# A seventh V tile loaded in the middle of a fused attention-block kernel, with the homes of four operands exchanged

## The chip, the cores and the metric

The kernel runs on one core of a Trainium2 chip. The metric is the device time of one execution in microseconds (us), the median of three runs for the kernel before. One further execution was recorded by the profiler; all times of single instructions come from it, counted from the start of its span.

## The reference

The reference computes one decode step of a conditioned transformer block, and the gradients of its result. Cut to what matters:

```python
sa, ca, ga, sb, cb, gb = split(silu(c) @ w_mod, 6)          # 640 values each
h  = layernorm(x) * (1 + ca) + sa                           # x: 1 x 640
q  = (h @ wq)                                               # 32 heads x 192
p  = softmax(q . K * 192**-0.5)                             # K, V: 32 heads x 8192 x 192, bfloat16
x  = x + ga * ((p . V) @ wo)
h  = layernorm(x) * (1 + cb) + sb
x  = x + gb * mlp(h)       # x1 = h + const; x1 + gelu(layernorm(x1) @ w3) @ w4; w3: 640 x 1536, w4: 1536 x 640
out, and for a given grad_out the gradients of x, K, V, wq, wo, w3, w4, c, w_mod
```

K and V are 100 MB each, and so are their gradients dK and dV. For each head, dV is the outer product of the softmax row with the head's output gradient, and dK is the outer product of the score gradient dS with q. For dS the kernel needs the product of V with the output gradient, so V is read a second time.

## The kernel before, in words

**Tiles.** A head's K or V is handled as two tiles of 128 partitions x 32 rows x 192 values in bfloat16: 1536 KB each. The kernel has five K buffers (`KB`, 0 to 4), three V buffers (`VB`, 0 to 2), and `qs_bc`, the scaled queries of all heads on every partition, which is as large as a tile and is called `QT` when used as one. `pp` is a pool with one more buffer of that size, for products.

**First phase (to about 530 us).** A loop over 31 heads reads K and V of each head, makes scores, the softmax and the sums that the second phase needs.

**The middle (about 530 to 575 us).** The last head, the output projection, the MLP forward and backward. It is a long chain of small steps on all engines, written out by hand. In it `w3` is loaded into the product buffer (`wp`, L715) and its fifth row block into a `wo` buffer (`w3_4`); the rows of `w4` are loaded into `w4b` (blocks 0 to 3) and into `qs_bc` (blocks 4 to 11, L680). TensorE transposes `w3` block by block (`w3t`, L840), and the last of these transposes is the last reader of `w3`. `dg_part` (L533) reads all `w4` rows on VectorE; `h2_part` (L929) multiplies them with the activation `g_bf` on TensorE, 60 small matmuls, of which columns 0 and 1 are taken before the output gradient `dao` is known and columns 2 to 4 after it. `er` rows are the softmax rows, transposed and stored to a DRAM scratch `eT_d` (`e_rows_out`, L491 and L492), from which `load_er` (L367) brings 8 KB per tile back onto four partitions. Those of the first tile of the second phase (`er0`) are loaded into a free stretch of `qs_bc` (issued on the SP queue at 558.20), those of the second into a buffer of their own (`er_b`, 565.38). `m_add` (L481) is a small VectorE addition behind the `dao` chain; `er_b` lies where its operand `mt` was, so the load of `er_b` waits for it.

**The second phase (from 565 us).** A loop over 64 steps `s`, two tiles per head, from the last head down. A step makes dV of its tile from `er` and the head's output gradient (`dv_groups`: TensorE L1125, ScalarE copies L1126), and dK of its tile on VectorE (`dk_part`, L1130). For the next steps it multiplies the V tile with the output gradient (`mul_q`, L1095) and sums on TensorE (`tree_q`, L1114). Stores go out on the POOL queue (dV L1419, dK L1423), V tiles come in on the SP queue (L328), the er rows on the ACT queue. Outputs take turns in five buffers, V tiles in four:

```python
OB = (KC, VB[2], QT, KE, KD)                     # dV of step s: OB[2s % 5], dK: OB[(2s+1) % 5]
def v_buf(s):
    return KY if s == 0 else VB[2] if s == 1 else (VB[0], VB[1], KX, KY)[(s - 2) % 4]
```

V tiles 0 to 4 are in place or under way when the phase begins, tile 5 is loaded in two halves (L1433) as tile 0 is used up, and step `s` loads tile `s + 5` into the home of tile `s + 1` once that is multiplied. The order on TensorE, VectorE, ScalarE and SP is the order of the program text (a manual schedule); waits are put in by the tile framework wherever a buffer is written, read or given away. Weight gradients (`dw4`, dwo, dwq, dw_mod, dw3) and their loads (`wo` tiles L203, `wq` and `w_mod` chunks L1155) are placed between the steps by a plan written out by hand.

Of the kernel before, what the change touches and what calls it, by code (L numbers as in the profile page):

```python
# [8 lines left out]
FP32 = mybir.dt.float32  # L9
# [11 lines left out]
def kernel(  # L21
# [92 lines left out]
    def col(n, name, dtype=FP32):  # L114
        return const.tile([P, n], dtype, name=name)
# [238 lines left out]
    H1 = HQ - 1  # L354
    TL = NT - 1
    KX, KY, KC, KD, KE = (KB[(2 * HQ + k) % NKB] for k in (-4, -5, -3, -2, -1))
    OB = (KC, VB[2], QT, KE, KD)
    R8 = JH // 4
    NS = 2 * HQ

# [15 lines left out]
    with tc.tile_pool(name="vs", bufs=3) as vsp, tc.tile_pool(name="ft", bufs=2) as ft, \  # L376
# [161 lines left out]
        with tc.manual_schedule(engines=ORDER):  # L538
# [172 lines left out]
            score_tree(0, d1)  # L711
            score_mul(1, 1)
            score_tree(1, d1)
            wp = pp.tile([P, JH * DH], BF16, name="wp", tag="prod")
            nc.sync.dma_start(out=wp.rearrange("p (i n) -> p i n", i=4), in_=w3d[:, 0:4, :])  # L715
            dot_sum(d0, x["S"][:, 0:JH])
            o2 = pair_o(TL - 1, po)
# [5 lines left out]
            o_rows(H1 - 1, vy, op_y, 0, 16)  # L723
            w3_4 = wst.tile([P, F], BF16, name="w3_4", tag="wo")
            nc.sync.dma_start(out=w3_4, in_=w3d[:, 4, :])
            load_rows(qs_bc[:, 0 : 4 * D], 4, 8)
            load_rows(qs_bc[:, 4 * D : 8 * D], 8, 12)
            mx = row_max(x["S"])
            V_.tensor_copy(out=AO[:, :, 2 * TL - 2 : 2 * TL], in_=ps_ao)
            o_rows(H1 - 1, vy, op_y, 16, 48)  # L730
# [81 lines left out]
            ac = col(ND, "ac")  # L812
            V_.scalar_tensor_tensor(out=ac, in0=cb1, scalar=nm, in1=mo[:, 1, :], op0=ALU.mult, op1=ALU.add)
            e_rows_out(TL - 1, er_ps)
            e_rows_out(TL, er_ps2, qs_bc[:, 8 * D : 8 * D + P])
            er0 = load_er(0, nc.sync, qs_bc[:, 8 * D : 8 * D + R8 * P].rearrange("p (k q) -> p k q", q=P))
            v1, var2 = sc8[:, 8:9], sc8[:, 9:10]
            V_.scalar_tensor_tensor(out=v1, in0=va, scalar=r1[:, 0:1], in1=cov, op0=ALU.mult, op1=ALU.add)
            V_.scalar_tensor_tensor(out=var2, in0=v1, scalar=r1[:, 0:1], in1=k4[:, 3:4], op0=ALU.mult, op1=ALU.add)
# [104 lines left out]
            h2b = []  # L924

            def h2_part(lo, hi, a0=0, a1=NF):
                for k in range(lo, hi):
                    for a in range(a0, a1):
                        T_.matmul((h2_ps[:, k : k + 1] if k < 2 else h2b[0][:, k - 2 : k - 1]), lhsT=w4r(a)[:, k * P : (k + 1) * P], rhs=g_bf[:, a : a + 1], start=(a == 0), stop=(a == NF - 1))  # L929

            w3t()
            pe = m_units(3, ky[1], vs3, mp)
# [29 lines left out]
                    A_.activation(out=dst[:, (a - a0) * D : (a - a0 + 1) * D], in_=dbo_bc, func=ACT.Copy, scale=g_[:, a : a + 1])  # L962

            dw4s = w4b[:, 0 : 5 * D]
            dw4_act(dw4s, 0, 4, 5)
            dn_ps = psO.tile([P, 256], FP32, name="dn_ps", tag="op")[:, 0:ND]
            for a in range(NF):
                for k in range(ND):
# [18 lines left out]
            V_.tensor_tensor(out=Ag, in0=A1, in1=ga, op=ALU.mult)  # L987
            V_.scalar_tensor_tensor(out=B1, in0=vv, scalar=nr1, in1=dy_c, op0=ALU.mult, op1=ALU.add)
            V_.tensor_tensor(out=Bg, in0=B1, in1=ga, op=ALU.mult)
            pr = col(4 * ND, "pr").rearrange("p (a b) -> p a b", b=ND)  # L990
            V_.tensor_tensor(out=pr, in0=dn_ps[:, None, :].to_broadcast([P, 4, ND]), in1=G, op=ALU.mult)
            h2_part(0, 1, 0, 6)
            ps = mean_mm(pr.rearrange("p a b -> p (a b)"), 4 * ND)
            h2_part(0, 1, 6, NF)
            h2_part(1, 2)
            d_n2, vg = col(ND, "d_n2"), col(ND, "vg")
            V_.tensor_tensor(out=vg, in0=Ag, in1=dn_ps, op=ALU.mult)
            V_.tensor_tensor(out=vg, in0=vg, in1=Bg, op=ALU.add)
# [4 lines left out]
            V_.reduce_sum(out=qr, in_=q4.rearrange("p a b -> p b a"), axis=AX.X)  # L1003
            V_.tensor_tensor(out=dao_bf, in0=vg, in1=qr, op=ALU.add)
            V_.tensor_tensor(out=dao, in0=vg, in1=qr, op=ALU.add)
            m_add(H1 - 1, mp, mt)
            A_.copy(out=d_n2, in_=dn_ps)
            A_.copy(out=bo[:, 0:2], in_=h2_ps[:, 0:2])

            def dx1_out():  # L1010
                q = pr
# [15 lines left out]
                V_.tensor_scalar(out=x1, in0=mo[:, 0, :], scalar1=m0[:, 0:1], scalar2=None, op0=ALU.add)  # L1027


    cpr = col(HQ, "cpr")  # L1030
    ckS = col(NQ, "ckS")
    dha = col(ND, "dha")
# [30 lines left out]
                scale=rinv[:, h : h + 1],  # L1063
            )

    for t in (TL - 2, TL - 1):
        wo_l[t] = load_wo(t)
    er_l = {0: er0, 1: load_er(1, nc.sync)}

    def q_bc(h, pool=psB, tag="b"):  # L1070
        ps = pool.tile([P, 2 * P], FP32, name="q_ps", tag=tag)
# [5 lines left out]
    do_mm(TL, 1)  # L1077
    dw4_store(dw4s[:, 4 * D : 5 * D], 4, 1)
    dw4_act(dw4t, 5, 5, 6)
    h2b.append(psS.tile([P, 3], FP32, name="h2_pb", tag="s"))  # L1080
    h2_part(2, ND)
    cx = bst.tile([P, HQ, ND], FP32, name="v_bc")
    V_.tensor_tensor(out=cx, in0=AO.rearrange("p k h -> p h k"), in1=dao[:, None, :].to_broadcast([P, HQ, ND]), op=ALU.mult)
    cs = ckS[:, 0:HQ]
# [1 line left out]
    dw4_dve(dw4t, 5, 6, 7)  # L1086
    dw4_store(dw4t, 5, 2)
    qh = q_bc(H1, psT, "t")
    A_.copy(out=bo[:, 2:ND], in_=h2b[0])

    pq = pp.tile([P, 2, JQ, DH], BF16, name="pq", tag="prod")
    dao_bc = bst.tile([P, D], BF16, name="dao_bc")

    def mul_q(s, q):
# [168 lines left out]
    def g_small():  # L1263

        ck3 = ckS.rearrange("p (t b) -> p t b", b=3)
        V_.tensor_tensor(out=bo, in0=bo, in1=h_b, op=ALU.add)
        V_.tensor_tensor(out=ao, in0=aoP, in1=aoN, op=ALU.add)
        for b, h0 in ((0, 0), (2, 1)):
            V_.tensor_tensor(out=ck3[:, :, b], in0=M1[:, h0:HQ:2, DH], in1=cpr[:, h0:HQ:2], op=ALU.mult)
        for lo, hi, h0 in ((0, 64, 0), (64, P, 1)):  # L1270
            V_.tensor_tensor(out=ck3[lo:hi, :, 1], in0=M2[lo:hi, :, DH], in1=cpr[lo:hi, h0:HQ:2], op=ALU.mult)
        A_.mul(out=ckS, in_=ckS, mul=SCALE)
        V_.tensor_tensor(out=d_cb, in0=d_sb, in1=n1, op=ALU.mult)
        V_.tensor_tensor(out=d_ga, in0=dx1, in1=ao, op=ALU.mult)
# [112 lines left out]
        while prog[1] < NP and 4 * plan[prog[1]][0] <= prog[0] - 1:  # L1387
            step()

    def v_buf(s):  # L1390
        return KY if s == 0 else VB[2] if s == 1 else (VB[0], VB[1], KX, KY)[(s - 2) % 4]

    OL = [OB[i % 5] for i in range(2 * NS - 5)]
    OL += [v_buf(NS - 3), OB[3], v_buf(NS - 2), OB[4], v_buf(NS - 1)]
    v_l = {s: v_buf(s) for s in range(5)}
    assert ht(4) == (H1 - 2, 0) and v_buf(4) is KX
    dq_x = bst.tile([P, 3], FP32, name="dq_x")
    V_.memset(dq_x, 0.0)

# [61 lines left out]
    for s in range(NS):  # L1461
        h, t = ht(s)
        nxt = s + 1 < NS
        doh = do_of(h)
        dP = tcol(JH, "dP")
        dot_sum(ps, dP)
        dS4 = bst.tile([P, JH, 4], BF16, name="dS4", bufs=2)
        V_.scalar_tensor_tensor(
            out=dS4,
            in0=dP[:, :, None].to_broadcast([P, JH, 4]),  # L1470
            scalar=cpr[:, h : h + 1],
            in1=E_all[:, h, t * JH : (t + 1) * JH, None].to_broadcast([P, JH, 4]),
            op0=ALU.subtract,
            op1=ALU.mult,
        )
        dV, dK = OL[2 * s], OL[2 * s + 1]
        gs = [0, 1, 2, 3, 4, 5, 6, 7]
        if not nxt:
            gs = [0, 2, 4, 6, 1, 3, 5, 7]
        if s == 0:  # L1480
            gs = [None] * 8
        else:
            er = er_l.pop(s)
        if nxt:
            ps = psR.tile([P, JH, TS], FP32, name="dot_ps")

        def dv(k):
            if gs[k] is not None:
                dv_groups(dV, er, doh, (gs[k],))

        def tree(q, lo, hi):
            if nxt:
                tree_q(ps, s + 1, q, lo, hi)

        dv(0)
        dv(1)
        slot()
        tree(0, 0, 4)
        if nxt:
            mul_q(s + 1, 1)  # L1500
            half_q(s + 1, 1)
            v_l.pop(s + 1, None)
        if 0 < s < NS - 5:
            v_l[s + 5] = load_v(*ht(s + 5), v_buf(s + 5))
        dv(2)
        tree(0, 4, 8)
        dv(3)
        tree(0, 8, 12)
        dk_part(dK, qh, dS4, 0, JQ)
        if not nxt:  # L1510
            dv_store(s, dV, 0, JQ, nc.sync)
        if s in (0, NS - 1):
            dk_store(s, dK, 0, JQ)
        if s == 0:
            dw4_store(dw4s[:, 3 * D : 4 * D], 3, 1)
        slot()
        dv(4)
        tree(1, 0, 3)
        dk_part(dK, qh, dS4, JQ, JH)
        if s > 0 and late0:  # L1520
            late0.pop(0)()
        dk_store(s, dK, JQ if s in (0, NS - 1) else 0, JH)
        if row is not None:
            dq_cols(row)
            row = None
        dv(5)
        tree(1, 3, 6)
        slot()
        dv(6)
        tree(1, 6, 9)  # L1530
        dv(7)
        if s + 2 < NS:
            er_l[s + 2] = load_er(s + 2)
        if s == 0:
            pass
        elif nxt:
            dv_store(s, dV, 0, JH)
        else:
            dv_store(s, dV, JQ, JH, nc.sync)
        tree(1, 9, 12)  # L1540
        if h == H1:
            row = dq_rows(t, (KD, KE)[t], dS4)
        if s + 2 < NS:
            assert (s + 2) // 4 in done
            mul_q(s + 2, 0)
            half_q(s + 2, 0)
        if nxt and ht(s + 1)[0] != h:
            qh = q_bc(ht(s + 1)[0])
        done_s[0] = s + 1
        slot()  # L1550
# [32 lines left out]
```

## Time and profile before

| | |
|---|---|
| runs | 1386.55, 1388.25, 1389.93 us; median 1388.25 |
| profiled execution | 1387.89 us, its span 1386.1 us |
| busy: PE, DVE, ACT, POOL | 85%, 80%, 66%, 8% of the span |
| moved by DMA | 569.38 MB, 411 GB/s over the span |
| HBM read, written | 340.97 MB, 226.44 MB |

PE is TensorE, DVE VectorE, ACT ScalarE, POOL GpSimd, SP the engine that issues most loads. In the profile's rows a number in brackets is the idle time just before an instruction and what ended it. SPq and ACTq mark the issue of a transfer, not its end. In tables of stretches, each engine has its busy time and a count of instructions, PEclk is the share of TensorE's clock that was granted, and the last two columns are the busy share of the 16 DMA engines and the GB/s that they moved.

### The profile page before, as it was taken

The page shows a single profiled execution, that of the slowest core. Times are in us where ns is not written, and L with a number is a line of the kernel's source. Part 1 is how long each engine was busy: PE and PEld are TensorE (multiplying, and loading weights), DVE is VectorE, ACT ScalarE, POOL GpSimd, SP SyncE. Part 2 cuts the span into 40 slices and gives each one's busy share as a digit, 9 for nine tenths or more (in the row PEclk, how much of TensorE's full clock was granted, in tenths as well). Part 3 has the DMA queues.
Part 4 walks back from the last instruction along what each step waited for, and adds up shares of the span by engine and source line. Part 5 has one row for each costly group of instructions (what it writes and reads, how often), then busy time and mean ns, then how long its engine had stood idle before and what let it go on. Part 6 is the DMA issues. An engine that isn't in the chain of part 4 may idle for free.

```text
span 1386.1 us, 30498 instructions
## 1 busy us (share of the span) xinstructions
PE 1177.9 (85%) x12712; PEld 739.7 (53%) x12712; DVE 1111.0 (80%) x1459; ACT 910.1 (66%) x2003; POOL 108.5 (8%) x196
## 2 busy tenths in 40 slices
PE   3888999999999999989878799798778877878984
PEld 2777777777777778644323344344334343434431
DVE  4999999999999999988667587677677765877784
ACT  0777777777777778766556566566566565656654
POOL 0000000000000000111111011011011111111110
PEclk7899999999999999765555555555565565655555
DMA  9999999999999999799999999999999999999997
GB/s 382 389 415 415 419 423 425 407 426 421 421 415 423 406 421 384 286 413 423 422 424 419 422 410 428 425 420 426 422 408 421 417 423 422 397 420 417 424 416 336
DMA packets 76872, 569.38 MB, mean 411 GB/s; under 512 B 7422, under 2 KB 25198, under 8 KB 37182
## 3 DMA queue, kind: packets, MB, share of 16 engines
q1 hardware_dynamic: 51594, 342.03, 60.3%
q0 software_dynamic: 24624, 224.89, 38.8%
q8 instruction: 99, 1.62, 0.4%
q10 hardware_dynamic: 516, 0.51, 0.1%
q14 instruction: 39, 0.32, 0.1%
HBM read 340.97 MB, written 226.44 MB: 409 GB/s over the span
## 4 chain that ended last, share of the span: by engine, by line
issue 41%; DVE 24%; DMA 16%; PE 10%; POOL 5%; ACT 2%; POOLq 0%; SPq 0%; DVEq 0%; ACTq 0%
DMA KB<-in_A_k_cache_dram 10%; DVE prod L333 10%; DVE prod L337 5%; DMA out_dram<-KB 4%; DVE vs L403 3%; PE mp L425 2%; DMA out_dram<-VB 2%; POOL out_dram L1423 2%; PE half_ps L343 2%; POOL out_dram L1419 2%; PE mp L430 1%; PE dot_ps L1114 1%; POOL out_dram L1229 1%; DVE pq L1095 1%; ACT vs L410 1%
## 5 line engine op out<-in xcount | busy, mean ns | idle before, releaser
L1114 PE MATMUL dot_ps<-pq,ident_bf 128*128 128x256 bf16 x1494 | 377.4, 395 | 32.7 <-DVE dP L347 29.1
L1126 ACT CAST KB<-dv_ps 128x768 bf16<-128x768 f32 x312 | 242.9, 807 | 100.3 <-PE dv_ps L1125 99.4
L410 ACT ACTIVATE vs<-VB,Ef 128x192 bf16<-128x192 bf16 x840 | 303.6, 447 | 0.0
L1114 PEld LDWEIGHTS <-ident_bf 128*128 128x128 bf16 x1494 | 149.8, 123 | 185.4 <-issue 147.4
L1125 PE MATMUL dv_ps<-do_r,er_b 1*128 1x192 bf16 x2016 | 226.7, 336 | 4.2 <-ACT KB L1126 2.9
L333 DVE TENSOR_TENSOR prod<-KB,qs_bc 128x6144 bf16<-128x6144 bf16 x62 | 207.9, 3353 | 24.6 <-DMA KB<-in_A_k_cache_dram 20.8
L1130 DVE TENSOR_TENSOR KB<-qh,dS 128x3072 bf16<-128x3072 bf16 x74 | 128.1, 1752 | 101.1 <-DMA out_dram<-KB 91.6
L425 PE MATMUL mp<-vs,KB 128*128 128x193 bf16 x1984 | 189.3, 247 | 4.3 <-ACT vs L410 3.3
L425 PEld LDWEIGHTS <-KB 128*128 128x128 bf16 x1984 | 169.0, 98 | 13.4 <-issue 4.8
L1125 PEld LDWEIGHTS <-er_b 1*128 1x128 bf16 x2016 | 69.0, 104 | 148.1 <-issue 145.8
L904 ACT COPY wT<-wT_ps 128x1024 bf16<-128x1024 bf16 x82 | 79.3, 967 | 95.1 <-PE wT_ps L903 95.1
L343 PE MATMUL half_ps<-prod,ident_bf 128*128 128x256 bf16 x744 | 95.1, 279 | 43.2 <-DVE prod L337 43.2
L403 DVE TENSOR_TENSOR vs<-VB,E 128x1728 bf16<-128x1728 bf16 x120 | 123.7, 1051 | 0.3 <-ACT vs L410 0.3
L1095 DVE TENSOR_TENSOR pq<-VB,do_r 128x3072 bf16<-128x3072 bf16 x66 | 115.4, 1749 | 0.0
L337 DVE TENSOR_TENSOR prod<-prod 128x3072 bf16<-128x3072 bf16 x62 | 108.7, 1754 | 1.0
L1095 DVE TENSOR_TENSOR pq<-KB,do_r 128x3072 bf16<-128x3072 bf16 x62 | 108.5, 1749 | 0.0
L430 PE MATMUL mp<-vs,KB 128*64 128x193 bf16 x1968 | 105.7, 250 | 0.0
L343 PEld LDWEIGHTS <-ident_bf 128*128 128x128 bf16 x744 | 72.7, 99 | 61.5 <-issue 52.5
L1126 ACT CAST qs_bc<-dv_ps 128x768 bf16<-128x768 f32 x104 | 80.6, 805 | 31.2 <-PE dv_ps L1125 30.6
L390 ACT ACTIVATE E<-S_h,negm 128x256 bf16<-128x256 f32 x31 | 15.7, 508 | 114.1 <-DVE negm L561 111.8
L1126 ACT CAST VB<-dv_ps 128x768 bf16<-128x768 f32 x96 | 74.4, 807 | 24.4 <-PE dv_ps L1125 24.1
L430 PEld LDWEIGHTS <-KB 128*64 128x64 bf16 x1968 | 78.8, 109 | 19.9 <-issue 19.6
(383 smaller groups left out, 1214.3 us busy)
## 6 DMA issues: line engine op xcount, KB each, us to landing
VB<-in_A_v_cache_dram SPq DMA_DIRECT2D x93, 1536.0 KB
out_dram<-KB POOLq DMA_DIRECT2D x74, 1536.0 KB, 17.0
KB<-in_A_k_cache_dram SPq DMA_DIRECT2D x63, 1536.0 KB
KB<-in_A_v_cache_dram SPq DMA_DIRECT2D x29, 1536.0 KB
out_dram<-qs_bc POOLq DMA_DIRECT2D x25, 1536.0 KB, 16.4
out_dram<-VB POOLq DMA_DIRECT2D x25, 1536.0 KB, 16.6
wo_st<-in_A_wo_dram SPq DMA_DIRECT2D x31, 480.0 KB
w_st<-in_A_wq_dram SPq DMA_DIRECT2D x12, 960.0 KB
```

What stands on the lines that cost most here:

```text
L333: V_.tensor_tensor(out=prod, in0=src, in1=vec[:, None, :].to_broadcast([P, JH, DH]), op=ALU.mult)
L337: V_.tensor_tensor(out=prod[:, :, 0:HW], in0=prod[:, :, 0:HW], in1=prod[:, :, DH - HW : DH], op=ALU.add)
L343: T_.matmul(ps, lhsT=ident_bf, rhs=prod[:, :, k : k + TF], start=(k == 0), stop=(k == w - TF))
L403: V_.tensor_tensor(out=vs[:, 0:n, 0:DH].rearrange("p j (a b) -> p j a b", b=4), in0=v[:, v0 : v0 + n, :].rearrange("p j (a b) -> p j a b", ...
L410: A_.activation(out=vs[:, k, 0:DH], in_=v[:, v0 + k, :], func=ACT.Copy, scale=Ef[:, j0 + k : j0 + k + 1])
L425: T_.matmul(mp[:, 0:MW], lhsT=kb[:, j0 + k, 0:P], rhs=vs[:, k, 0:MW], start=(q == 0 and k == 0), stop=(z and k == JQ - 1), skip_group_chec ...
L430: T_.matmul(mp[p0 : p0 + 64, MO : MO + MW], lhsT=kb[:, j0 + k, P:DH], rhs=vs[:, k, 0:MW], start=False, stop=(z and k >= JQ - 2), skip_grou ...
L1095: V_.tensor_tensor(out=pq[:, q], in0=v_l[s][:, q * JQ : (q + 1) * JQ, :], in1=do_of(ht(s)[0])[:, None, :].to_broadcast([P, JQ, DH]), op=AL ...
L1114: T_.matmul(ps[:, q * JQ : (q + 1) * JQ, :], lhsT=ident_bf, rhs=pq[:, q, :, k : k + TS], start=(k == 0), stop=(k == w - TS), skip_group_ch ...
L1125: T_.matmul(ps[:, b, k * DH : (k + 1) * DH], lhsT=er[p0 : p0 + 1, 2 * m + k, :], rhs=doh[p0 : p0 + 1, :], start=True, stop=True)
L1126: A_.copy(out=dV4[:, 2 * q : 2 * q + 2, m * PW : (m + 1) * PW], in_=ps[:, :, 0:PW])
L1130: V_.tensor_tensor(out=dK[:, lo:hi, :].rearrange("p j (a b) -> p j a b", b=4), in0=qh.rearrange("p (a b) -> p a b", b=4)[:, None, :, :].to ...
```

## The change

- `w3` is loaded into `qs_bc` (home of q), and `w4` blocks 4 to 11 into the product buffer (`pq`, now allocated in the middle): the two exchange homes.
- Once the last transpose has read `w3`, the seventh V tile (`s = 6`) is loaded into `qs_bc`, between the loads of the two `wo` tiles. Step 1 of the second phase then loads no V tile.
- The homes are rotated: `qs_bc` joins the V buffers in place of `VB[0]`, and `VB[0]` the output buffers: `OB = (KC, VB[2], KE, VB[0], KD)`. V tile 2 still lies in `VB[0]`.
- `er0` is no longer loaded early into `qs_bc`: it goes with the second tile's, into an `er_b` buffer, issued behind the V tile and the second `wo` tile. For this `m_add` moves ahead of the `dao` chain's last steps.
- `h2_part` is divided by rows, not by columns: blocks 4 to 7 for all five columns before `dao`, the other eight blocks after it, into a second PSUM tile, copied to `bo2` and added later. One `dw4_act` (ScalarE) moves behind the copy of `bo`.

```diff
-    OB = (KC, VB[2], QT, KE, KD)
+    OB = (KC, VB[2], KE, VB[0], KD)
...
-            wp = pp.tile([P, JH * DH], BF16, name="wp", tag="prod")
+            pq = pp.tile([P, 2, JQ, DH], BF16, name="pq", tag="prod")
+            pqf = pq.rearrange("p a j d -> p a (j d)")
+            wp = qs_bc
             nc.sync.dma_start(out=wp.rearrange("p (i n) -> p i n", i=4), in_=w3d[:, 0:4, :])
...
-            load_rows(qs_bc[:, 0 : 4 * D], 4, 8)
-            load_rows(qs_bc[:, 4 * D : 8 * D], 8, 12)
+            load_rows(pqf[:, 0, 0 : 4 * D], 4, 8)
+            load_rows(pqf[:, 1, 0 : 4 * D], 8, 12)
...
-            e_rows_out(TL, er_ps2, qs_bc[:, 8 * D : 8 * D + P])
-            er0 = load_er(0, nc.sync, qs_bc[:, 8 * D : 8 * D + R8 * P].rearrange("p (k q) -> p k q", q=P))
+            e_rows_out(TL, er_ps2, pqf[:, 0, 4 * D : 4 * D + P])
...
-            def h2_part(lo, hi, a0=0, a1=NF):
+            def h2_part(ps, rows, lo=0, hi=ND):
                 for k in range(lo, hi):
-                    for a in range(a0, a1):
+                    for a in rows:
...
-            dw4_act(dw4s, 0, 4, 5)
...
+            m_add(H1 - 1, mp, mt)
             pr = col(4 * ND, "pr").rearrange("p (a b) -> p a b", b=ND)
             V_.tensor_tensor(out=pr, in0=dn_ps[:, None, :].to_broadcast([P, 4, ND]), in1=G, op=ALU.mult)
-            h2_part(0, 1, 0, 6)
+            h2_part(h2_ps, range(4, 8), 0, 2)
             ps = mean_mm(pr.rearrange("p a b -> p (a b)"), 4 * ND)
-            h2_part(0, 1, 6, NF)
-            h2_part(1, 2)
+            h2_part(h2_ps, range(4, 8), 2, ND)
...
-            m_add(H1 - 1, mp, mt)
             A_.copy(out=d_n2, in_=dn_ps)
-            A_.copy(out=bo[:, 0:2], in_=h2_ps[:, 0:2])
+            A_.copy(out=bo, in_=h2_ps[:, 0:ND])
+            dw4_act(dw4s, 0, 4, 5)
...
-    for t in (TL - 2, TL - 1):
-        wo_l[t] = load_wo(t)
-    er_l = {0: er0, 1: load_er(1, nc.sync)}
+    def v_buf(s):
+        return KY if s == 0 else VB[2] if s == 1 else VB[0] if s == 2 else (QT, VB[1], KX, KY)[(s - 2) % 4]
+
+    wo_l[TL - 2] = load_wo(TL - 2)
+    v_l = {s: v_buf(s) for s in range(5)}
+    v_l[6] = load_v(*ht(6), v_buf(6))
+    wo_l[TL - 1] = load_wo(TL - 1)
+    er_l = {t: load_er(t, nc.sync) for t in (0, 1)}
...
-    h2b.append(psS.tile([P, 3], FP32, name="h2_pb", tag="s"))
-    h2_part(2, ND)
+    h2b = psS.tile([P, ND], FP32, name="h2_pb", tag="s")
+    h2_part(h2b, (0, 1, 2, 3, 8, 9, 10, 11))
...
-    A_.copy(out=bo[:, 2:ND], in_=h2b[0])
+    A_.copy(out=bo2, in_=h2b)
...
+        V_.tensor_tensor(out=bo, in0=bo, in1=bo2, op=ALU.add)
...
-        if 0 < s < NS - 5:
+        if 1 < s < NS - 5:
             v_l[s + 5] = load_v(*ht(s + 5), v_buf(s + 5))
```

More of the change, by code (lines that the diff above doesn't have):

```diff
@@ L922 @@
             h2_ps = psO.tile([P, 256], FP32, name="h2_ps", tag="op")
-            h2b = []
-            def h2_part(lo, hi, a0=0, a1=NF):
+            def h2_part(ps, rows, lo=0, hi=ND):
                 for k in range(lo, hi):
-                    for a in range(a0, a1):
-                        T_.matmul((h2_ps[:, k : k + 1] if k < 2 else h2b[0][:, k - 2 : k - 1]), lhsT=w4r(a)[:, k * P : (k + 1) * P], rhs=g_bf[:, a : a + 1], start=(a == 0), stop=(a == NF - 1))
+                    for a in rows:
+                        T_.matmul(ps[:, k : k + 1], lhsT=w4r(a)[:, k * P : (k + 1) * P], rhs=g_bf[:, a : a + 1], start=(a == rows[0]), stop=(a == rows[-1]))
             w3t()
@@ L1027, in d_sb_out @@
                 V_.tensor_scalar(out=x1, in0=mo[:, 0, :], scalar1=m0[:, 0:1], scalar2=None, op0=ALU.add)
+    bo2 = col(ND, "bo2")
     cpr = col(HQ, "cpr")
@@ L1064, in do_mm @@
             )
-    for t in (TL - 2, TL - 1):
-        wo_l[t] = load_wo(t)
-    er_l = {0: er0, 1: load_er(1, nc.sync)}
+    def v_buf(s):
+        return KY if s == 0 else VB[2] if s == 1 else VB[0] if s == 2 else (QT, VB[1], KX, KY)[(s - 2) % 4]
+    wo_l[TL - 2] = load_wo(TL - 2)
+    v_l = {s: v_buf(s) for s in range(5)}
+    assert ht(4) == (H1 - 2, 0) and v_buf(4) is KX
+    v_l[6] = load_v(*ht(6), v_buf(6))
+    wo_l[TL - 1] = load_wo(TL - 1)
+    er_l = {t: load_er(t, nc.sync) for t in (0, 1)}
     def q_bc(h, pool=psB, tag="b"):
@@ L1088 @@
     qh = q_bc(H1, psT, "t")
-    A_.copy(out=bo[:, 2:ND], in_=h2b[0])
-    pq = pp.tile([P, 2, JQ, DH], BF16, name="pq", tag="prod")
+    A_.copy(out=bo2, in_=h2b)
     dao_bc = bst.tile([P, D], BF16, name="dao_bc")
@@ L1388, in slot @@
             step()
-    def v_buf(s):
-        return KY if s == 0 else VB[2] if s == 1 else (VB[0], VB[1], KX, KY)[(s - 2) % 4]
     OL = [OB[i % 5] for i in range(2 * NS - 5)]
     OL += [v_buf(NS - 3), OB[3], v_buf(NS - 2), OB[4], v_buf(NS - 1)]
-    v_l = {s: v_buf(s) for s in range(5)}
-    assert ht(4) == (H1 - 2, 0) and v_buf(4) is KX
     dq_x = bst.tile([P, 3], FP32, name="dq_x")
```

## The prediction

> **What bounds the kernel now.** First the page's slices, since the change moves a transfer: the busy share of the DMA engines and the rate, 34.65 us to a slice.
>
> ```profile
> DMA  9999999999999999799999999999999999999997
> GB/s 382 389 415 415 419 423 425 407 426 421 421 415 423 406 421 384 286 413 423 422 424 419 422 410 428 425 420 426 422 408 421 417 423 422 397 420 417 424 416 336
> ```
>
> The DMA engines are full before and after the middle; the one hole is slice 16, with a little of 15. From about 590 us every stretch of 8 us that I asked for has a share of 0.96 or more until 1364, so the second phase ends when its bytes are moved. Next, the table by stretches of 5 us, to see where the hole lies and what runs beside it.
>
> ```profile
> 550.00:555.00 5.00, 5.00 (x120) 4.75 (x118) 4.69 (x19) 4.46 (x14) 1.07 (x2) 1.00 0.87 305
> 555.00:560.00 5.00, 4.78 (x77) 4.56 (x74) 4.93 (x25) 4.31 (x6) 0.00 (x0) 1.00 0.30 110
> 560.00:565.00 5.00, 4.40 (x116) 3.72 (x114) 4.14 (x28) 4.86 (x8) 0.00 (x0) 0.93 0.61 195
> 565.00:570.00 5.00, 4.17 (x61) 3.19 (x62) 4.90 (x8) 4.28 (x11) 1.27 (x2) 0.50 0.57 179
> 570.00:575.00 5.00, 4.43 (x30) 3.19 (x29) 4.60 (x9) 4.10 (x7) 1.33 (x2) 0.50 1.01 356
> 575.00:580.00 5.00, 4.80 (x28) 3.12 (x24) 5.00 (x4) 2.47 (x4) 1.63 (x3) 0.50 1.01 415
> 580.00:585.00 5.00, 4.71 (x71) 2.98 (x70) 4.96 (x5) 2.89 (x5) 0.53 (x1) 0.86 1.00 410
> 585.00:590.00 5.00, 4.65 (x78) 3.14 (x76) 4.97 (x8) 4.84 (x8) 0.53 (x1) 1.00 0.97 351
> ```
>
> From 555 to 570 the DMA moves 161 GB/s on average, some 40% of its full rate. But look at the third engine column, DVE: from 575 to 590 VectorE is busy 5.00, 4.96, 4.97 of 5 us, and 585 to 590 moves only 351 GB/s. There VectorE sets the pace, and the DMA just keeps up. Last, the timelines of SP, POOL and the engines around the changed steps.
>
> ```profile
> 550.75 0.34 SPq L328 DMA_DIRECT2D KB<-in_A_v_cache_dram  x1
> 558.20 0.59 SPq L367 DMA_DIRECT2D qs_bc<-eT_d  x1
> 558.90 2.75 SPq L203 DMA_DIRECT2D wo_st<-in_A_wo_dram  x2
> 565.38 0.50 SPq L367 DMA_DIRECT2D er_b<-eT_d  x1
> 584.35 10.02 SPq L328 DMA_DIRECT2D VB<-in_A_v_cache_dram  x2
> 587.96 0.53 POOL L1423 DMA_DIRECT2D out_dram<-KB  x1 [7.13 <-DVE KB L1130]
> 563.37 0.18 DVE L991 TENSOR_TENSOR pr<-dn_ps,G 128x20 f32<-128x20 f32 x1 [0.33 <-PE dn_ps L969]
> 566.77 0.97 PE L1125 MATMUL dv_ps<-do_r,qs_bc 1*128 1x192 bf16 x8
> 567.52 2.91 ACT L1126 CAST KB<-dv_ps 128x768 bf16<-128x768 f32 x4
> 572.13 0.19 DVE L1451 SCALAR_TENSOR_TENSOR cpr<-c_ps,rinv 128x32 f32<-128x32 f32 x1 [0.33 <-PE c_ps L1448]
> ```
>
> The first L328 row is V tile 4; the pair at 584.35 is tile 6, which the change moves, and tile 7. The store at 587.96 is dK of step 1. At 566.77 TensorE uses `er0`, loaded long before.
>
> **What the tile is worth at most.** The kernel's first loads queue on SP behind each other. They show a queue's order and the price of a tile: TensorE waits for `wq` until 11.32, VectorE for the K tile behind it until 15.07.
>
> ```profile
> 1.20 0.42 SPq L239 DMA_DIRECT2D wm_a<-in_w_mod_dram  x1
> 7.56 1.36 PE L233 MATMUL mod_ps<-sc_bf,wm_a 128*128 128x1 bf16 x45 [0.46 <-DMA wm_a<-in_w_mod_dram]
> 11.32 1.76 PE L260 MATMUL q_ps<-w_st,ha_bf 128*128 128x384 bf16 x5 [1.61 <-DMA w_st<-in_A_wq_dram]
> 15.07 3.36 DVE L333 TENSOR_TENSOR prod<-KB,qs_bc 128x6144 bf16<-128x6144 bf16 x1 [4.55 <-DMA KB<-in_A_k_cache_dram]
> ```
>
> So 1536 KB (1.573 MB) cost 3.75 us in a full queue (0.42 MB/us). If the hole took the tile and no new hole opened, the gain is 3.75 us.
>
> **Where a new hole opens.** What is queued until 590? At 570 there remain, of the `wq` chunk (0.98 MB), two `dw4` stores (0.16, 0.33) and the first half of V tile 5 (0.79), less the 179 GB/s x 5 us = 0.90 MB moved, 1.36 MB. Until 588 are issued: the other half of tile 5, dV and dK of step 0 in halves, `dw4` (0.49 and 0.16), V tile 6 and dK of step 1: 7.75 MB. From 570 to 590 the table moves (356 + 415 + 410 + 351) x 5 = 7.66 MB. So at 590 1.45 MB are left, less than one tile: tile 6 and dK of step 1 were the only work left from about 585 on. Without tile 6 the queue runs dry there, until the store of 587.96 moves its first bytes, about 1 us after its issue (the `wo` load issued at 558.90 moves 35 GB/s from 559 to 560, then 273). At 590 this store would have 1.573 - 1 x 0.42 = 1.15 MB left. The gain is the difference, 0.30 MB: **0.75 us**, not 3.75. From 590 on the backlog grows (8.5 MB issued or left by 600, 4.1 moved), so nothing later opens a gap, and any delay of the VectorE chain that leads to dK of step 1 adds to the end in full.
>
> **What delays that chain.** The tile can be issued when the last transpose has read `w3`: the second `wo` load waits for the same transposes and is issued at 561.3 (the group of two ends at 561.65). `er0` is issued after `m_add`, at about 563.4, on the same queue behind tile 6 and a `wo` tile. A load of 1.47 MB into an empty queue took 1.20 to 7.56, 6.36 us until TensorE could use it. By that row tile 6 is there at 561.3 + 6.36 + 0.24 (for 0.10 MB more) = 567.9, the `wo` tile 0.49 / 0.42 = 1.2 later, `er0` with it: **569.1**. Before, ScalarE's first cast began at 567.52, some 0.55 behind a TensorE start that could have been 567.0. So TensorE stands 2.1 us. Behind its waiting L1125 matmuls are queued `tree_q`, `do_mm` and the matmul for `cpr`; VectorE waits for `cpr` (572.13, with 0.33 idle already) before anything of step 1. **Delay 2.1 us.**
>
> The Trainium skill says the same of the order (DMA: Bandwidth & Descriptors, Queues, rings and completion order): a queue's descriptors are consumed in ring order on each DMA engine. It speaks against this change. Its fixed cost (same page, Anatomy of one DMA: about 2.0 us plus bytes at 436 GB/s, measured for GpSimd's path) would put tile 6 at 566.9, `er0` at 568.0 and the sum at +0.3.
>
> Bounds of the delay: below, nothing, if `er0` is let past the tile; above, a small load's whole latency behind the data. The smallest loads took 1.65 (end of issue) to 4.76, 3.1 us; V tile 4, issued at 550.75, had left the DMA at about 556.3, 5.5 us, which puts the data of tile 6 and `wo` at 568.0 and `er0` at 571.1, a delay of 4.1. I take 2.1, since `wq` and K above came one transfer time behind each other, with no latency added.
>
> **Edits that I cost at nothing.** `m_add` (0.35 us) goes into the 0.33 us that VectorE waits before L991; uncovered, 0.35. `h2_part` has 60 matmuls in both; after `dao` 40 for 36 at 1.13 us, 0.13 more, beside TensorE's stand for `er0`. `dw4_act` (0.84 us) ends at about 565.5, before `do_r` at 565.93 (0.65 idle there); uncovered, 0.4. The load of `w3` waits only for VectorE, 537.5 instead of 539.10, into a DMA with a share of 0.99: nothing. The first `wo` load no longer waits behind `er0` (558.20): nobody waits for it. The new `bo` addition, 0.16 us, falls at 612, where compute is ahead of the DMA. dV of step 1 goes to `KE`, whose last reader stands ahead of it on TensorE; dK of step 1 to `VB[0]`, whose last reader is ahead of it on VectorE. From V tile 7 on loads, stores and waits are those of before under other names.
>
> **Sum.** -0.75 + 2.1 = +1.35 us, against the execution's own 1387.89: 1389.2. That execution stands 0.36 below the median of 1388.25, so on the median's scale **1389.6**.
>
> **Rivals.**
> 1. *The hole is filled and stays filled* (faster): `er0` costs nothing and stores of step 0 keep the DMA busy until 588. For it: slice 16, and a second phase that ends with its bytes. Against it: the 351 GB/s of 585 to 590 with tile 6 still in the sum. 1388.25 - 3.75 = 1384.5.
> 2. *`er0` pays its latency behind the data* (slower): delay 4.1, and with the new hole the credit of 0.75 is gone too, if dK's first bytes are as late as the first of `wo`. 1388.25 + 4.1 = 1392.3. It decides from where TensorE's first L1125 starts after about 570.5 (a delay of 3.5, less 0.75: +2.8). For it: SP's small transfers have not been seen behind a full tile in an empty stage; the store of 32 KB to the same scratch took 7.2 us to land. Against it: the cadence of the first loads.
> 3. *The order doesn't bind*: `er0` sits on four partitions and lands before the rest of the tile. Only the 0.75 us remain: 1387.5.
>
> **How the numbers follow.** About 0.2%, 2.8 us, is what a measurement of this kernel can tell from no change. The forecast (delay 1 to 3.5) has a chance of 0.43, rival 3 0.10; both lie within 0.2%: 0.53. Rival 2 has 0.34: the stage has no row for a small load behind a tile, and each edit that I cost at nothing has a price above nothing if its cover fails, none below. Rival 1 has 0.13. The range runs from 1385.2, which takes in half of rival 1, to 1393.0, past rival 2; the forecast's own is 1387.5 to 1391.
>
> **What would show it.** Right: a tile issued at about 561.3, the stretches 560 to 570 nearly full, a new hole between about 586 and 591, the first L1125 of `dv_ps` at about 569 behind a DMA release, `cpr` at about 574.2 and dK of step 1 at about 590 instead of 587.96. Wrong: L1125 at 567 (the chain does not move), no hole at 586, or dK's store after 591.5. A second phase of another length, counted from dK of step 1, would mean that the rotation of homes costs something that I have put at nothing.

## The result, and the profile after

| | before | after |
|---|---|---|
| median of 13 runs each, on one chip | 1387.87 us | 1395.57 us |
| lowest to highest | 1382.19 to 1389.93 | 1392.29 to 1405.27 |
| profiled execution, its span | 1387.89, 1386.1 | 1392.29, 1390.5 |

The ratio is 1.0067, with a 95% interval of 1.0051 to 1.0082: slower by some 0.7%, where 1389.6 us and "within 0.2%" had been forecast, and outside the range. The profiled execution is the fastest of the thirteen, so its span shows only 4.4 us of the loss.

The slices of the page of after, 34.76 us each, the same two rows as were shown of before:

```profile
DMA  9999999999999999889999999999999999999998
GB/s 371 391 418 416 416 412 421 409 419 417 414 413 415 400 420 392 318 352 423 421 420 420 425 418 423 424 423 425 419 421 423 422 418 419 413 414 419 424 413 339
```

The DMA engines are as busy as before, and the page counts the same packets. But in slices 3 to 13, which lie in the first phase, where no instruction was changed, the rates are 416 416 412 421 409 419 417 414 413 415 400, mean 413.8; before had 415 419 423 425 407 426 421 421 415 423 406, mean 418.3. That is 1.1% less.

The table by stretches of 5 us around the middle of after (the columns are those of the same table of before):

```profile
565.00:570.00 5.00, 4.22 (x105) 3.70 (x102) 4.28 (x28) 4.40 (x9) 0.27 (x1) 0.88 0.73 246
570.00:575.00 5.00, 2.65 (x54) 2.04 (x53) 4.71 (x6) 2.78 (x6) 1.00 (x2) 0.50 0.97 352
...
585.00:590.00 5.00, 3.48 (x57) 2.03 (x55) 4.96 (x5) 2.31 (x4) 1.45 (x3) 0.84 0.96 379
590.00:595.00 5.00, 5.00 (x47) 3.25 (x45) 4.97 (x7) 3.33 (x5) 0.53 (x1) 0.73 0.13 50
```

The hole between 560 and 570 is partly filled, and there is a new one: 590 to 595 moves 50 GB/s while VectorE is busy 4.97 of 5 us. The timelines of SP, POOL and the other engines of after, at the rows that the prediction had shown of before:

```profile
561.40 0.34 SPq L203 DMA_DIRECT2D wo_st<-in_A_wo_dram  x1
565.40 0.33 SPq L328 DMA_DIRECT2D qs_bc<-in_A_v_cache_dram  x1
565.83 0.58 SPq L203 DMA_DIRECT2D wo_st<-in_A_wo_dram  x1
567.63 1.12 SPq L367 DMA_DIRECT2D er_b<-eT_d  x2
567.21 0.35 DVE L481 TENSOR_TENSOR M<-mp,mt 64x193 f32<-64x193 f32 x1
567.59 0.18 DVE L990 TENSOR_TENSOR pr<-dn_ps,G 128x20 f32<-128x20 f32 x1
573.15 0.82 PE L1129 MATMUL dv_ps<-do_r,er_b 1*128 1x192 bf16 x8 [1.73 <-DMA er_b<-eT_d]
578.35 0.19 DVE L1451 SCALAR_TENSOR_TENSOR cpr<-c_ps,rinv 128x32 f32<-128x32 f32 x1 [2.28 <-PE c_ps L1448]
594.18 0.53 POOL L1423 DMA_DIRECT2D out_dram<-VB  x1 [7.13 <-DVE VB L1134]
600.28 0.33 SPq L328 DMA_DIRECT2D VB<-in_A_v_cache_dram  x1
```

Lines have moved by up to 4 (L1125 is L1129). `pr` stands at 567.59 instead of 563.37, so all behind it comes 4.22 us later. Taken back to the scale of before by those 4.22: tile 6 is issued at 561.2, TensorE starts `dv_ps` at 568.9 behind a DMA release, `cpr` comes at 574.1, dK of step 1 is stored at 590.0, and the hole lies at 585.8 to 590.8.

So the span is made up of three pieces: 4.22 us more up to `pr`, 2.00 more from there to dK of step 1 (26.59 instead of 24.59), and 1.82 less from that store to the end (796.3 instead of 798.1). The middle does what the prediction said. The first piece is where nothing was said at all. 3.95 of its 4.22 us are already there in the first `L649`, the row maximum of the last head's scores, where the middle begins. Before, and after:

```profile
528.46 0.22 DVE L649 TENSOR_REDUCE m<-S_h 128x1 f32<-128x64 f32 x1
```

```profile
532.41 0.22 DVE L649 TENSOR_REDUCE m<-S_h 128x1 f32<-128x64 f32 x1
```

**What differs in the first phase.** One line of the change touches it, `bo2 = col(ND, "bo2")`. It takes a column of 20 bytes per partition out of the pool of constants, rounded up to 32. The pools are laid out behind one another, so all that lies behind the constants moves up by 32 bytes: temporaries, weight tiles, V buffers, the product buffer, K buffers and the small buffers of the second phase. Before, K, V and product tiles begin at multiples of 4096 bytes of a partition (V at 94208, K at 143360), after at 94240 and 143392. `qs_bc` and the result columns, among the constants, stay where they were.

### The profile page after: what moved, and what is told of

It reads as the page before. It is cut to its first block, busy times and chain, and to the rows that moved or that the text cites. A ratio compares the mean times of both kernels' runs of the same rounds, so it can differ in the third digit from the quotient of the medians.

```text
span 1390.5 us, 30498 instructions
## 1 busy us (share of the span) xinstructions
PE 1184.0 (85%) x12712; PEld 742.7 (53%) x12712; DVE 1111.0 (80%) x1460; ACT 910.2 (65%) x2003; POOL 108.2 (8%) x196
## 4 chain that ended last, share of the span: by engine, by line
issue 46%; DVE 24%; DMA 14%; PE 8%; POOL 6%; ACT 1%; SPq 0%; POOLq 0%; DVEq 0%; ACTq 0%
DVE prod L333 10%; DMA KB<-in_A_k_cache_dram 9%; DVE prod L337 5%; DVE vs L403 3%; DMA out_dram<-VB 3%; PE mp L425 3%; POOL out_dram L1423 2%; POOL out_dram L1419 2%; PE half_ps L343 2%; PE mp L430 1%; POOL out_dram L1233 1%; DMA w_st<-in_A_wq_dram 1%; DVE pq L1099 1%; DMA KB<-in_A_v_cache_dram 1%; DVE S_h L347 1%
## 5 line engine op out<-in xcount | busy, mean ns | idle before, releaser
L410 ACT ACTIVATE vs<-VB,Ef 128x192 bf16<-128x192 bf16 x840 | 303.5, 447 | 0.0
L1129 PE MATMUL dv_ps<-do_r,er_b 1*128 1x192 bf16 x2048 | 230.3, 336 | 7.0 <-ACT KB L1130 4.7
L333 DVE TENSOR_TENSOR prod<-KB,qs_bc 128x6144 bf16<-128x6144 bf16 x62 | 207.8, 3352 | 26.8 <-DMA KB<-in_A_k_cache_dram 19.1
L1130 ACT CAST VB<-dv_ps 128x768 bf16<-128x768 f32 x200 | 155.8, 804 | 58.4 <-PE dv_ps L1129 53.7
L425 PE MATMUL mp<-vs,KB 128*128 128x193 bf16 x1984 | 189.5, 247 | 4.7 <-ACT vs L410 3.3
L425 PEld LDWEIGHTS <-KB 128*128 128x128 bf16 x1984 | 168.9, 98 | 14.0 <-DMA KB<-in_A_k_cache_dram 5.9
L1129 PEld LDWEIGHTS <-er_b 1*128 1x128 bf16 x2048 | 70.7, 104 | 153.0 <-issue 151.0
L1134 DVE TENSOR_TENSOR VB<-qh,dS 128x3072 bf16<-128x3072 bf16 x52 | 89.7, 1753 | 59.7 <-DMA out_dram<-VB 59.7
L347 DVE TENSOR_REDUCE dP<-dot_ps 128x32 f32<-128x512 f32 x64 | 43.9, 686 | 47.2 <-PE dot_ps L1118 46.7
```

What stands on the lines that cost most here:

```text
L333: V_.tensor_tensor(out=prod, in0=src, in1=vec[:, None, :].to_broadcast([P, JH, DH]), op=ALU.mult)
L410: A_.activation(out=vs[:, k, 0:DH], in_=v[:, v0 + k, :], func=ACT.Copy, scale=Ef[:, j0 + k : j0 + k + 1])
L425: T_.matmul(mp[:, 0:MW], lhsT=kb[:, j0 + k, 0:P], rhs=vs[:, k, 0:MW], start=(q == 0 and k == 0), stop=(z and k == JQ - 1), skip_group_chec ...
L1129: T_.matmul(ps[:, b, k * DH : (k + 1) * DH], lhsT=er[p0 : p0 + 1, 2 * m + k, :], rhs=doh[p0 : p0 + 1, :], start=True, stop=True)
L1130: A_.copy(out=dV4[:, 2 * q : 2 * q + 2, m * PW : (m + 1) * PW], in_=ps[:, :, 0:PW])
L1134: V_.tensor_tensor(out=dK[:, lo:hi, :].rearrange("p j (a b) -> p j a b", b=4), in0=qh.rearrange("p (a b) -> p a b", b=4)[:, None, :, :].to ...
```

## The experiments

Theory A: the loss is the 32 bytes, and costs in the first phase; the rest of the change is worth what the prediction summed (+0.1%). Theory B: the loss is in the reordered middle (the wait for `er0`, the hole, or the rotated homes). Each kernel was timed in five rounds beside the kernel before. Kernels told of in one section shared a chip unless the text says otherwise, and "first L649" is the row above, read in each kernel's trace (L651 where the edit adds two lines ahead of it).

### The change without its new column, and the column without the change

```diff
-    bo2 = col(ND, "bo2")
+    bo2 = hx          # e1: a column that is no longer read
```

> The changed kernel with one line undone: bo2 is put into a column that is dead by then (hx), so that the constants take no 32 bytes more and every buffer behind them (V, K, product, weights) has the address of before. Address theory (the 32 bytes slow the transfers of all tiles): what remains is the late er0 and the moved hole, +2.0 - 0.75, so 1388.5 to 1390, ratio to before 1.001 (0.999 to 1.002). Schedule theory (rotation of homes or the new order costs the time, the address nothing): 1394 to 1397, ratio 1.005 or more.

The kernel before, with an unused column that is only set to zero:

```diff
+    pad = col(5, "pad")
+    V_.memset(pad, 0.0)
```

> The kernel before with nothing but an unused constant of 5 columns ahead of the pools, which takes the 32 bytes that bo2 takes, and one memset of it (0.06 us). Address theory: 1393 to 1395, ratio 1.004 to 1.006, with the first phase longer by about 4 us and the second by about 3. Schedule theory: no change, 1387 to 1389, ratio 0.999 to 1.001.

Measured: the change with the old addresses 1389.57 us, ratio 1.0013 [0.9997, 1.0030]; the kernel before with the new addresses 1395.15, ratio 1.0056 [1.0036, 1.0076]. Theory A holds in its main point and theory B falls: the reordered middle is worth +0.13%, and 32 bytes in a kernel in which nothing else is changed are worth +0.56%. The first L649 of the unchanged kernel with its 32 bytes:

```profile
534.64 0.22 DVE L649 TENSOR_REDUCE m<-S_h 128x1 f32<-128x64 f32 x1
```

and that of the change without them:

```profile
527.78 0.22 DVE L649 TENSOR_REDUCE m<-S_h 128x1 f32<-128x64 f32 x1
```

Where do the six microseconds go? One stretch, 60 to 500 us, of the table by stretches (busy time of PE, PEld, DVE, ACT, POOL, then clock, DMA share and GB/s), for the kernel before:

```profile
60.00:500.00 440.00, 403.41 (x6242) 339.54 (x6241) 417.57 (x415) 328.84 (x1072) 8.23 (x15) 1.00 1.01 417
```

and for the same kernel 32 bytes off:

```profile
60.00:500.00 440.00, 399.66 (x6156) 336.18 (x6155) 412.03 (x409) 327.02 (x1067) 8.27 (x15) 1.00 1.01 412
```

The clock is full and the DMA share is full in both. TensorE, VectorE and ScalarE get through 0.5 to 1.4% fewer instructions in the same time, and the DMA moves 412 instead of 417 GB/s: 1.2% of 440 us is 5.3 us. The engines' own instructions are not slower. VectorE's costliest operation of this phase, which reads K and writes the product buffer, in the groups of before:

```profile
L333 DVE TENSOR_TENSOR prod<-KB,qs_bc 128x6144 bf16<-128x6144 bf16 x62 | 207.9, 3353 | 24.6 <-DMA KB<-in_A_k_cache_dram 20.8
```

and 32 bytes off:

```profile
L333 DVE TENSOR_TENSOR prod<-KB,qs_bc 128x6144 bf16<-128x6144 bf16 x62 | 207.8, 3352 | 26.6 <-DMA KB<-in_A_k_cache_dram 22.8
```

3353 and 3352 ns; in this row only the wait for the load of K has grown, from 20.8 to 22.8 us. The costliest groups of ScalarE and TensorE in this phase agree as well: 447 and 447 ns (L410), 247 and 248 ns (L425). The bytes are the same, the engines are not slower, and the DMA, busy throughout, moves fewer bytes per us: the time is lost in the loads.

### How far off

The kernel before with the unused column of 64 and of 128 bytes (`col(16, "pad")`, `col(32, "pad")`), and with all buffers 256 bytes lower, by giving eight temporary columns one buffer instead of two:

```diff
     def tcol(n, name, dtype=FP32):
+        if name in ("S6", "sk", "s4", "rm", "x2", "d_n0", "dx", "dc_t"):
+            return tmp.tile([P, n], dtype, name=name, bufs=1)
```

> The kernel before with an unused constant of 16 columns: all buffers behind it move by 64 bytes. Address theory with a boundary of 64 bytes: no change, ratio 0.999 to 1.001; with a boundary of 128 bytes or more: as with 32 bytes, ratio 1.003 to 1.006. Schedule theory: no change.

> The kernel before with an unused constant of 32 columns: all buffers behind it move by 128 bytes. The moves by 32 and by 64 bytes both cost 0.56%. If the boundary that matters is 128 bytes: no change, ratio 0.999 to 1.001, first phase (first L649 of the middle) at 526 to 529. If it is 256 bytes or more: ratio 1.004 to 1.007, first L649 at 532 to 535.

> The kernel before with eight one-use scratch columns kept single instead of double, so that all buffers behind them lie 256 bytes lower; the program is the same otherwise. Boundary of 256 bytes or less: no change, ratio 0.999 to 1.001. Boundary of 512 bytes or more (the tiles of before begin at multiples of 4096): as with 32 bytes, ratio 1.004 to 1.007. Any other cause of the cost of e2 and e3 (the unused constant itself, its memset): no change here, as none is there.

| off by | median us | ratio [95%] | first L649 |
|---|---|---|---|
| 0 (before; on the chip of +32 and +64, of +128 and -256) | 1386.40, 1385.62 | 1 | 528.46 |
| +32 | 1395.15 | 1.0056 [1.0036, 1.0076] | 534.64 |
| +64 | 1394.89 | 1.0057 [1.0035, 1.0079] | 532.27 |
| +128 (on another chip) | 1392.58 | 1.0040 [1.0023, 1.0056] | 530.96 |
| -256 (the same chip as +128) | 1384.91 | 0.9989 [0.9973, 1.0005] | 528.05 |

256 bytes lower cost nothing, although no tile starts at a multiple of 4096 any more. Any of 32, 64 and 128 costs the same within the intervals. The boundary that counts is 256 bytes. Not every detail came as expected: the second phase was to be some 3 us longer at +32, and that run does not show it (798.0 us from dK of step 1 to the end, 798.1 before); at +128 the first L649 was to stand at 532 to 535. The ratios with their intervals differ from the quotients of two medians by up to 0.12% (1.0056 beside 1.0063 at +32).

The Trainium skill has this boundary (DMA: Bandwidth & Descriptors, How a descriptor splits into AXI transactions): a transfer goes in pieces of 256 bytes, each starting at a multiple of 256, and one that starts off the boundary also fetches the bytes below it, which are not used and cost beats. The section does not say whether this holds for a load's destination in the core's memory, which is what moved here. The runs agree that the boundary is 256. By that section's beats of 32 bytes a tile's row of 12288 bytes takes 384 beats, at +32 one more, at +64 two and at +128 four more: an estimate of 0.26%, 0.5% and 1.0% of the loads, from that section of the Trainium skill. Of the 528 us until the first L649 that would be 1.4, 2.8 and 5.5 us. In the traces the first L649 came 6.2 us later than before at +32 (3.5 in the second run of that kernel, below), 3.8 at +64 and 2.5 at +128: more than the estimate at +32, less than half of it at +128, and no growth with the offset. Counted in the same section's pieces instead of its beats, a row takes 49 for 48 at any offset, an estimate of 2.1% or 11 us; that would not grow with the offset, but it is more than any trace lost.

### Which buffer pays

Five kernels move parts of the memory. In the first only the K buffers and what lies behind them move (a pad of 32 bytes in the product's pool):

```diff
+    pad = pp.tile([P, 8], FP32, name="pad", tag="pad")
+    V_.memset(pad, 0.0)
```

> The kernel before with the 32 bytes put behind the V buffers and the product buffer: only the K buffers and the second phase's small buffers move. If each misplaced transfer pays for itself: about half of the first phase's 4 to 5 us, first L649 at 530 to 531, and a ratio of 1.002 to 1.003. If only the V buffers matter: no change. If one misplaced stream slows the whole queue: as e2, 1.0056.

The next two: V and product off, all else at multiples of 256 as before (the version 256 bytes lower, with pads of 32 bytes ahead of V and 224 behind the product); product and K off (a pad behind V).

```diff
+    for pool, n in ((wst, 8), (pp, 56)):          # on top of the version at -256
+        pad = pool.tile([P, n], FP32, name="pad", tag="pad", bufs=1)
+        V_.memset(pad, 0.0)
```

> The kernel before with every buffer 256 bytes lower (the version that cost nothing, ratio 0.9989), and on top of that only the V tiles' home and the product tile behind it 32 bytes off a multiple of 256; the K tiles' home, the weight tiles and the small tiles stay on multiples of 256. Theory A, the V loads pay (they are the larger half of the first phase's tiles that land in one home): ratio 1.004 to 1.006 against the kernel before, first L649 at 531 to 535 us. Theory B, the price belongs to the small homes (weights, temporaries) or needs all of them together: ratio 0.999 to 1.002, first L649 at 526 to 528.5 us.

```diff
+    pad = vp.tile([P, 8], FP32, name="pad")
```

> The kernel before with 32 bytes of padding behind the V tiles' home, so that the product tile and the K tiles' home are 32 bytes off and the V tiles' home, the weights and the temporaries stay. Theory A, the V loads pay: ratio 0.999 to 1.002, first L649 at 526 to 528.5 us. Theory C, the product tile pays (VectorE and TensorE read and write it in every step of the first phase): ratio 1.004 to 1.006, and the run with V and product off shows the same.

The last three: weight tiles and temporaries off, V, product and K in place (on top of -256, pads of 32 bytes behind the constants and 224 behind the weights); V, product and K off, weights and temporaries in place (a pad of 32 behind the weights); and the run of all off once more, as an anchor on the same chip.

```diff
+    for pool, n in ((const, 8), (wst, 56)):       # e11, on top of the version at -256
...
+    pad = wst.tile([P, 8], FP32, name="pad", tag="pad", bufs=1)          # e12
```

> The kernel before with the weight tiles (the homes of w_st and wo_st) 32 bytes off a multiple of 256 and the small temporaries moved by 32 bytes or a little less; V, product, K and everything behind them stay. Theory B1, the price belongs to the weight homes or the temporaries: ratio 1.004 to 1.006, first L649 at 531 to 535 us. Theory B2, it needs K and V tiles off together: 0.999 to 1.002, first L649 at 526 to 528.5 us.

> The kernel before with the V tiles' home, the product tile, the K tiles' home and the small pool behind it 32 bytes off; the weight homes and the temporaries stay. Theory B1: 0.999 to 1.002. Theory B2: 1.004 to 1.006 and a late first L649 (531 to 535 us). If the parts merely add, from the runs of the parts (V with product 0.9994, product with K 1.002, K 1.0007): 1.001 to 1.003.

> The kernel of the run with everything behind the constants 32 bytes off, again, beside the two partial ones on the same chip. If the size of the effect is a matter of the placement alone: 1.0036 to 1.0076 as before. If it belongs to the chip or hour of the earlier comparison: 0.999 to 1.002, and then the partial runs of this and the last comparison say nothing about which buffer pays.

| off by 32 | median us | ratio [95%] | first L649 |
|---|---|---|---|
| K (and behind it) | 1387.39 | 1.0007 [0.9989, 1.0024] | 527.15 |
| V, product | 1384.97 | 0.9994 [0.9978, 1.0011] | 527.98 |
| product, K | 1389.33 | 1.0020 [1.0003, 1.0037] | 529.40 |
| weights, temporaries | 1389.06 | 1.0015 [0.9997, 1.0032] | 528.51 |
| V, product, K | 1389.39 | 1.0021 [1.0001, 1.0041] | 529.38 |
| all, again | 1395.08 | 1.0053 [1.0035, 1.0071] | 531.97 |

K went with the versions at +128 and -256; the second and third shared a third chip, the last three a fourth. The effect is the same on each chip that was asked (1.0056 and 1.0053 for the same kernel). The kernel before had medians of 1385.62, 1386.07 and 1386.21 on these three chips. A pad and its memset are not the cause by themselves: the K version has a pad of the same size and costs 0.07%. No buffer pays it alone: theories that gave it to V, to the product buffer or to the weights fell one after the other, and so did the one that needed only K and V together (1.004 to 1.006 expected, 1.0021 measured). The two halves, 0.15% and 0.21%, add up to 0.36%, and with their intervals to the whole 0.53% as well, so I can't say whether the parts merely add or whether all of them off together cost more. The table of the same stretch, 60 to 500 us, for the last two, which ran on one chip: V, product and K off,

```profile
60.00:500.00 440.00, 402.81 (x6224) 339.18 (x6224) 416.03 (x415) 327.66 (x1069) 8.25 (x15) 1.00 1.01 416
```

and all off:

```profile
60.00:500.00 440.00, 400.85 (x6202) 337.60 (x6202) 414.30 (x413) 328.56 (x1070) 8.23 (x15) 1.00 1.01 414
```

416 and 414, beside 417 of before. That alone would look like steps, but kernels whose buffers stand on the boundary differ as well (418 and 419 in the two traces of the next section). The kernel before and its shifted versions, one profile of each:

| buffers | first L649 | from dK of step 1 to the end | GB/s, 60 to 500 us | GB/s, 650 to 1350 us |
|---|---|---|---|---|
| before; -256 | 528.46; 528.05 | 798.1; 795.4 | 417; 418 | 419; 420 |
| parts off (five kernels) | 527.15 to 529.40 | 795.2 to 799.3 | 416 to 419 | 418 to 421 |
| all off: +32, again, +64, +128 | 534.64, 531.97, 532.27, 530.96 | 798.0, 800.8, 796.1, 799.2 | 412, 414, 414, 415 | 419, 417, 421, 419 |

In the first phase the kernels with all buffers off stand apart in both columns, and those with parts off hardly differ from before. In the second phase the rate is the same in all three rows, so no loss of the first phase's size is seen there; the times scatter too much to exclude two or three us. The first L649 is late by 2.5 to 6.2 us, while the ratios stand for 5.5 to 7.9 us, so where the rest is lost is not located. At +128 some of it lies in the middle: from the first L649 to dK of step 1 that trace takes 62.87 us, before 59.50.

### The wait for er0, with the addresses of before

The change without its column, and tile 6's load put behind the second `wo` tile and both loads of er rows:

```diff
     wo_l[TL - 2] = load_wo(TL - 2)
-    v_l[6] = load_v(*ht(6), v_buf(6))
     wo_l[TL - 1] = load_wo(TL - 1)
     er_l = {t: load_er(t, nc.sync) for t in (0, 1)}
+    v_l[6] = load_v(*ht(6), v_buf(6))
```

> e1 with the seventh V tile issued behind both er loads instead of ahead of them (SP: wo, wo, er0, er1, V tile). er0 is then issued at about 563.4 into an idle queue (times on the scale of before) and lands 3.1 us later, at 566.5 to 567.5. Queue theory: the first L1129 of TensorE starts at about 567 instead of 569, dK of step 1 goes out as in the kernel before, and the moved hole leaves a gain of 0.75: 1387 to 1388, ratio 0.999 to 1.000, about 2 us below e1. If er0 is not what holds the second phase back: as e1.

Measured 1388.17 us, ratio 1.0010 [0.9991, 1.0029]. In the trace the wait is gone. First the change without its column, then this version:

```profile
561.91 0.33 SPq L328 DMA_DIRECT2D qs_bc<-in_A_v_cache_dram  x1
564.09 0.18 DVE L990 TENSOR_TENSOR pr<-dn_ps,G 128x20 f32<-128x20 f32 x1
564.13 1.12 SPq L367 DMA_DIRECT2D er_b<-eT_d  x2
569.56 0.82 PE L1129 MATMUL dv_ps<-do_r,er_b 1*128 1x192 bf16 x8 [1.63 <-DMA er_b<-eT_d]
590.59 0.53 POOL L1423 DMA_DIRECT2D out_dram<-VB  x1 [7.13 <-DVE VB L1134]
```

```profile
561.38 0.18 DVE L990 TENSOR_TENSOR pr<-dn_ps,G 128x20 f32<-128x20 f32 x1
561.42 1.12 SPq L367 DMA_DIRECT2D er_b<-eT_d  x2
562.59 0.44 SPq L328 DMA_DIRECT2D qs_bc<-in_A_v_cache_dram  x1
564.46 0.97 PE L1129 MATMUL dv_ps<-do_r,er_b 1*128 1x192 bf16 x8
585.64 0.53 POOL L1423 DMA_DIRECT2D out_dram<-VB  x1 [7.13 <-DVE VB L1134]
```

TensorE starts without a wait, and dK of step 1 comes 4.95 us earlier. Of these, 2.71 stand already in `pr` (1.40 of them in the first L649, 526.38 for 527.78), ahead of the wait. The other 2.24 are the wait: from `pr` to dK of step 1 it is 26.50 us with it and 24.26 without, and 24.59 in the kernel before. Most of the hole goes with it. First the change without its column, then this version:

```profile
585.00:590.00 5.00, 5.00 (x37) 2.97 (x36) 5.00 (x4) 2.67 (x5) 0.00 (x0) 0.59 0.40 162
```

```profile
585.00:590.00 5.00, 4.16 (x73) 2.73 (x74) 4.91 (x13) 4.67 (x9) 1.07 (x2) 1.00 0.75 317
```

The store of dK stands 5 us earlier in the second table, so the stretches are not quite alike. Over the same 5 us around each store (from 4.2 before it to 0.8 behind) the DMA moves 44 GB/s with the wait and 329 without, beside 335 in the kernel before.

So the queue behind tile 6 is the cause of the wait, as the prediction said. What that is worth in time is not shown: the two medians lie 1.4 us apart, less than the intervals. But against the kernel before there is nothing left of the tile either: +0.10%, with an interval that excludes the 3.75 us (-0.27%) that the tile was worth at most.

Last, the same with `qs_bc`, which lies 224 bytes past a multiple of 256 before and after and now takes V tiles, brought onto a multiple (`dao` allocated ahead of it):

```diff
+    dao = col(ND, "dao")     # ahead of qs_bc
...
-    dao = col(ND, "dao")     # behind it
```

> e4 with one 20-byte constant allocated ahead of qs_bc instead of behind it, so that qs_bc, which is now a V buffer of 14 tiles, begins at a multiple of 256 bytes (18944 instead of 18912) and all else stays. If the price of a misplaced tile load in the first phase (4 to 5 us over some 124 tiles, 0.04 us) holds: 0.5 us less than e4, 1386 to 1388, ratio to before 0.998 to 1.001; e8 is the version that should be no slower than the kernel before.

1386.77 us, ratio 1.0007 [0.9992, 1.0021] on the chip of -256. That is no measurable gain; the loads into `qs_bc` fall into the second phase, where no loss by the offset was seen. No version here beats the kernel before by more than its measurement is uncertain.

## Why the prediction was wrong, step by step

- **The step that failed is "Edits that I cost at nothing".** It costed the new `bo` addition as 0.16 us of VectorE beside other work. The trace has that addition at 0.17 us, at 618.77 and not at 612, and the change with the old addresses has it too, so it is not the loss. But its second operand was a new column, and the column's place in memory was not counted at all: 0.53 to 0.56% in the two runs of the kernel before with the same 32 bytes, 7 to 8 us. What the runs showed in place of nothing is a load phase that ends 3.5 to 6.2 us later (3.95 in the changed kernel) when the homes of all K, V and weight tiles stand 32 bytes off a multiple of 256. No rival had it, and the range ended at 1393.0.
- **The forecast without that term** was 1389.6, +0.10% on the median before. The change with the old addresses gave 1389.57, +0.13% [-0.03, +0.30], on a chip on which the kernel before had 1386.40. That the two times agree to 0.03 us is luck, and the interval does not tell +0.10% from no change. The two runs together, 0.13 and 0.56%, make up the 0.67% of the result within its interval.
- **Delay of the chain.** Forecast: `er0` behind tile 6 and `wo`, TensorE at 569.1, `cpr` late by 2.1. On the scale of before: 568.9, 2.0; the version that takes `er0` out of the queue removes 2.24. That the transfers come in the order of their queue held; rival 2's 4.1 us behind the data did not come, and rival 3 (`er0` lands before the tile) fell too.
- **The new hole.** Forecast between 586 and 591, on that scale 585.8 to 590.8, with 50 GB/s. So rival 1, in which the hole is filled and stays filled, fell as well. The stretches of 560 to 570 were to be nearly full; the two of after that answer to them, 565 to 575, moved 246 and 352 GB/s for 195 and 179 before, so that was half right.
- **The credit of 0.75 us** can't be told: from dK of step 1 to the end single profiles of the kernel before and its shifted versions took 795.2 to 800.8, after 796.3, the change with old addresses 799.0. Nor did the rotation of homes show a cost.
- **The covers.** `m_add` filled the idle 0.33 us ahead of `pr` exactly: 0.35 at 567.21, and `pr` follows without a wait.
- **What would have shown the mistake.** The prediction named the first L1125, `cpr` and the hole in absolute times. It did not name the start of the middle, which should have stood at 528 and stood at 532.

## What to carry to other kernels

A new small buffer has a place as well as an instruction. Where pools are laid out behind one another, a column of 20 bytes moves every tile behind it, so compare the buffers' addresses, not only the instructions, before an edit is costed at nothing, and keep the homes of large transfers at multiples of 256 bytes. Here a new column could take over a dead one. When a kernel is slower, look first for the earliest row that is late: here it stood ahead of the first instruction that was changed, and none of the reasons that the change had been argued about could reach it.

## What the hardware showed

- A kernel whose first phase is bound by its loads lost 0.53 to 0.57% when its buffers stood 32 or 64 bytes past a multiple of 256, 0.40% at 128, and nothing at 256. The DMA engines' share stays at 1.0; only the rate tells it (412 to 415 instead of 417 or 418 GB/s).
- In the second phase, in which nearly all of the 226 MB are written, the same offsets show no lower rate (417 to 421 beside 419 and 420 GB/s). Why the first phase pays and the second does not is not shown.
- What remains open is how the price is shared between the buffers, why it doesn't grow from 32 to 128 bytes, and where the part of it falls that the first phase's traces don't show.
